# Transposed exponentials through DRAM blocks and VectorE, and a new order of the first weights

The kernel runs on one core of a Trainium2 chip. The metric is the device time of one launch in microseconds (us); lower is better. Every time below is the median of several runs of the same kernel, and all runs were in the fast state (granted TensorE clock between 0.993 and 1.000 of full speed; the clocks below 0.996 are those of two runs of `after_again`). TensorE is PE in the profile, VectorE is DVE, ScalarE is ACT, and SyncE (SP, its queue SPq) only issues DMAs.

## The reference

A block-recurrent cross attention feeds a two-layer network. There are 8 batches and 8 heads of 64, 512 tokens `x` and 32 states per head.

```python
a      = softmax(scale * x @ state.T)      # 512 x 32 per head: every token reads the states
xread  = a @ state
a2     = softmax(scale * state @ x.T)      # 32 x 512 per head: every state reads the tokens
sread  = a2 @ x
t      = concat(xread, sread)              # (8 batches) x 544 rows x 512
h      = t @ w_in                          # 512 x 2048
g      = h * sigmoid(1.702 * h)
out    = g @ w_out                         # 2048 x 512
```

## The kernel before

The two weights arrive as 64-bit words and are turned into 32-bit floats on the chip, in 32 pieces of 512 KB (16 of `w_in`, 16 of `w_out`). Most of that is VectorE's work. For a `w_in` piece two of the steps, the "clamps", are on ACT; for a `w_out` piece all seven are on VectorE.

```python
PIECES = [("i", c, k) for c in range(NFC) for k in range(NPR)] + [("o", f) for f in range(NF)]
...
def round_a(i):
    if i not in power:
        mask(i)                                    # VectorE, and the source of the ACT clamps
    sc = power[i]
    if PIECES[i][0] == "o":
        nc.vector.tensor_scalar(sc, sc, most, least, ALU.min, ALU.max)
        nc.vector.tensor_scalar(sc, sc, -least, 8.0, ALU.add, ALU.mult)
        return
    nc.scalar.activation(out=sc.bitcast(FP32), in_=sc, func=AF.Relu, bias=edge[0], scale=-8.0)
    nc.scalar.activation(out=sc, in_=sc.bitcast(FP32), func=AF.Relu, bias=edge[1], scale=-1.0)
```

`powers_to(n)` does the clamps up to piece n; `rounds(n)` and `round_to(n)` finish pieces.

Batches 0 and 1 run while the weights are still arriving, with plain products: first `M = state @ w_in`, then "up products" `a @ M` with the gelu on ACT (that is `xread @ w_in`, summed over 8 x 32 states rather than 512 columns), and then a "down loop" of 16 steps, one `w_out` piece each. Batches 2 to 7 run later with a two-level Strassen scheme (fewer products, many additions on VectorE) and are TensorE-bound. The first such stage, which multiplies batch 1's gelus by `w_out`, lies between about 166 and 200 us.

The state's own read needs its exponentials `e` transposed. For batches 0 and 1 TensorE did it:

```python
att_s_exp(0, room[:, :NG]); att_s_exp(1, room[:, NG:])     # four 128x512 exponentials on ACT
rounds(1)                                                   # finish one weight piece
att_s_norm(0); att_s_norm(1)                                # 1/sum, and e = e * (1/sum), on VectorE
...
for f in range(NF):                                         # the down loop
    rounds(1)
    round_to(NFC * NPR + f + 1)
    for r in range(SCH):
        down(0, r, [f], out_x[0, r], r == SCH - 1)
    if f == 0:
        for b in range(2):
            for g in range(NG):
                att_eT(b, g)        # 4 TensorE transposes and an ACT copy
    if f == 1:
        att_sread(0); att_sread(1)
        ...
```

Batches 2 to 7 already did it another way: `eT_out` writes the exponentials to DRAM as 32x32 blocks, `eT_in` reads the blocks back at their new places, and `eT_turn` turns each block on VectorE.

## Time and profile before

| | before |
|---|---|
| median time of 3 runs | 708.97 us (708.93 to 709.03) |
| profiled span | 706.9 us |
| first exponential of batches 0 and 1 starts | 73.07 us |
| first product of the TensorE-bound part (`upx<-aT,M`) | 204.43 us |

The last row is my yardstick in every trace: from there on all kernels here do the same work at TensorE's pace, so what it moves by is, within about 0.3 us, what the whole time moves by.

ACT's timeline of the kernel before (start, duration, engine, line, operation, what it writes and reads, and in brackets the idle time before it and who ended it).

```profile
24.52 0.72 ACT L218 ACTIVATE low<-low,edge 128x512 f32<-128x512 int32 x1 [0.33 <-DVE low L207]
...
28.14 0.73 ACT L218 ACTIVATE low<-low,edge 128x512 f32<-128x512 int32 x1
```

Each line is the first clamp of a pair. They are done here, in front of the exponential of batch 1, in time that ACT would otherwise have spent waiting.

### The profile page before, as it was taken

How to read it: one execution, taken by the hardware profiler on the slowest of the kernel's cores; microseconds unless marked ns; L12 is line 12 of the kernel's file. 1: busy time of each engine (PE TensorE's matmuls, PEld its weight loads, DVE VectorE, ACT ScalarE, POOL GpSimd, SP SyncE). 2: the span in 40 equal slices, each digit the busy share in tenths (PEclk: the TensorE clock that was granted, in tenths of full speed). 3: DMA queues.
4: the chain of work that ended last, by engine and by line, in shares of the span. 5: the costliest groups of instructions: out<-in, count | busy, mean ns of one | idle time of the engine just before them, and what ended most of it. 6: DMA issues, size and time to landing. Idle time of an engine off the chain costs nothing.

```text
span 706.9 us, 12667 instructions
## 1 busy us (share of the span) xinstructions
PE 694.9 (98%) x4973; PEld 558.1 (79%) x4975; DVE 602.4 (85%) x1246; ACT 230.8 (33%) x456; POOL 0.8 (0%) x8
## 2 busy tenths in 40 slices
PE   8989999999999999999999999999999999999996
PEld 3433544458998799879988899889987998899995
DVE  6999799999978998799978996899789987888650
ACT  5686520014224413433243423342243124200210
POOL 0000000000000000000000000000000000000000
PEclk9999999999999999999999999999999999999999
DMA  8921246228742384309550765047432940041001
GB/s 230 368 74 54 93 146 154 115 89 206 213 118 37 61 194 145 69 9 206 148 105 1 152 182 120 16 82 199 137 51 48 194 148 16 0 125 57 16 1 29
DMA packets 143914, 77.89 MB, mean 110 GB/s; under 512 B 113904, under 2 KB 127728, under 8 KB 143856
## 3 DMA queue, kind: packets, MB, share of 16 engines
q1 hardware_dynamic: 143856, 77.09, 42.3%
q8 instruction: 39, 0.64, 0.4%
q14 instruction: 19, 0.16, 0.1%
HBM read 61.08 MB, written 15.99 MB: 109 GB/s over the span
## 4 chain that ended last, share of the span: by engine, by line
PE 95%; ACT 2%; DMA 2%; SPq 0%; DVE 0%; issue 0%; DVEq 0%
PE low L689 21%; PE o L1051 17%; PE o L738 14%; PE o L689 10%; PE o L542 8%; PE h L524 7%; PE upx L1051 6%; PE M L320 4%; PE o L585 2%; PE o L320 1%; PE sr L500 1%; PE warm L125 1%; PE upx_sr L1051 1%; DMA out_dram<-osb_sr 1%; DMA xn<-in_x_dram 1%; ACT low L219 1%
## 5 line engine op out<-in xcount | busy, mean ns | idle before, releaser
L1061 DVE TENSOR_TENSOR g<-o,g 128x512 f32<-128x512 f32 (+1 forms) x140 | 88.0, 650 | 51.1 <-PE o L1051 50.1
L738 PE MATMUL o<-w_out,g 128*128 128x256 f32 x448 | 100.6, 381 | 0.0
L738 PEld LDWEIGHTS o<-w_out,g 128*128 128x128 f32 x448 | 84.4, 190 | 16.6 <-issue 5.5
L1058 ACT ACTIVATE g<-g 128x512 f32<-128x512 f32 (+1 forms) x84 | 49.8, 600 | 100.9 <-DVE g L1061 100.9
L1051 PE MATMUL upx<-aT,M 128*128 128x256 f32 x192 | 49.3, 379 | 0.0
L1051 PE MATMUL o<-ta,M 128*128 128x256 f32 x192 | 49.3, 379 | 0.0
L1051 PE MATMUL o<-ta,ms 128*128 128x256 f32 x192 | 48.3, 379 | 0.0
L689 PE MATMUL low<-low,g 128*128 128x128 f32 x336 | 44.4, 275 | 0.0
L689 PEld LDWEIGHTS low<-low,g 128*128 128x128 f32 x336 | 40.9, 192 | 0.0
L460 ACT COPY M<-M 128x512 f32<-128x512 f32 x64 | 33.1, 598 | 22.7 <-PE M L320 22.7
L1051 PEld LDWEIGHTS o<-ta,ms 128*128 128x128 f32 x192 | 36.6, 190 | 4.9
L1051 PEld LDWEIGHTS o<-ta,M 128*128 128x128 f32 x192 | 36.6, 190 | 4.9
L1051 PEld LDWEIGHTS upx<-aT,M 128*128 128x128 f32 x192 | 36.1, 191 | 4.6
L689 PE MATMUL low<-sums,later 128*128 128x128 f32 x280 | 37.0, 275 | 0.0
L689 PEld LDWEIGHTS low<-sums,later 128*128 128x128 f32 x280 | 34.6, 192 | 0.4
L320 PE MATMUL M<-w_in,stT 64*32 64x512 f32 x512 | 31.9, 594 | 0.0
L527 ACT ACTIVATE g<-h 128x512 f32<-128x512 f32 x24 | 14.0, 591 | 54.7 <-PE h L524 54.7
L524 PE MATMUL h<-low,M 128*128 128x512 f32 x64 | 29.6, 597 | 1.5 <-DVE low L408 1.5
L524 PE MATMUL h<-aT,M 128*128 128x512 f32 x64 | 28.7, 599 | 1.4 <-ACT M L460 1.4
L689 PE MATMUL low<-w_out,g 128*128 128x128 f32 x224 | 29.6, 275 | 0.0
L542 PE MATMUL o<-w_out,g 128*128 128x512 f32 x64 | 28.6, 594 | 0.0
L542 PE MATMUL o<-w_out,sums 128*128 128x512 f32 x64 | 28.3, 593 | 0.0
(210 smaller groups left out, 1295.2 us busy)
## 6 DMA issues: line engine op xcount, KB each, us to landing
low<-low SPq DMA_DIRECT2D x78, 256.0 KB, 3.8
later<-in_moe_w_out_dram SPq DMA_DIRECT2D x16, 512.0 KB, 3.6
xn<-in_x_dram SPq DMA_DIRECT2D x28, 256.0 KB, 4.8
low<-low SPq DMA_DIRECT2D x9, 768.0 KB, 4.0
w_out<-in_moe_w_in_dram SPq DMA_DIRECT2D x12, 512.0 KB
xsq<-in_x_dram SPq DMA_DIRECT2D x96, 64.0 KB, 2.3
out_dram<-osb SPq DMA_DIRECT2D x18, 256.0 KB, 3.1
out_dram<-later SPq DMA_DIRECT2D x14, 256.0 KB, 2.2
```

The source lines that it names most:

```text
L125: nc.tensor.matmul(ps, zeros[:, :P], zeros, start=True, stop=True)
L320: nc.tensor.matmul(ps[g][st], A[b]["stT"][rows, st], rhs(rows, j), start=True, stop=True)
L460: nc.scalar.copy(m[:, g], ps[g])
L524: nc.tensor.matmul(hps, lhs[i], rhs[i], start=(i == 0), stop=(i == n - 1))
L527: nc.scalar.activation(out=G[key, f // 2][:, f % 2, :ntok], in_=hps, func=AF.Gelu_apprx_sigmoid)
L542: nc.tensor.matmul(ops, G[key, f // 2][:, f % 2, P * r : P * (r + 1)], w_out[:, f], start=(f == 0), stop=(f == NF - 1))
L585: nc.tensor.matmul(ps[:, r], lhs[f][:, P * r : P * (r + 1)], rhs[:, f], start=(first and r == 0 and f == 0), stop=(f == HF - 1), skip_grou ...
L689: nc.tensor.matmul(ps, lhs[f], rhs[:, f], start=(first and f == 0), stop=(f == QF - 1), skip_group_check=True)
L738: nc.tensor.matmul(ps[:, r], lhs[f][:, P * r : P * (r + 1)], rhs[:, f], start=(r == 0 and f == 0), stop=(f == HF - 1), skip_group_check=True,)
L1051: nc.tensor.matmul(ps[:, k], lhs[i][:, o : o + P], rhs[i], start=(first and k == 0 and i == 0), stop=(i == n - 1), skip_group_check=True,)
L1058: nc.scalar.activation(out=dst, in_=src, func=AF.Gelu_apprx_sigmoid)
L1061: nc.vector.tensor_tensor(out=dst, in0=ps, in1=x, op=ALU.add)
```

## The change

It has two parts, which touch different stretches.

- **The start.** Pieces of `w_in` become (chunk of 512 columns, half of the columns, two row blocks) rather than (chunk, row block), so that two pieces are enough for the first two up products. Some warm-up products go, some gelus are held back, and the clamps of two pieces move behind the exponential of batch 1.
- **The transposes.** Batches 0 and 1 take the road of the later ones: 16 transposes and 4 ACT copies go; 16 DMAs of 128 KB and four 128x512 transposes on VectorE come. The scaling by 1/sum moves from VectorE's `e * (1/sum)` to ACT's copy of the read.

The diff, cut (`...`) to its core:

```diff
-    PIECES = [("i", c, k) for c in range(NFC) for k in range(NPR)] + [("o", f) for f in range(NF)]
+    PIECES = [("i", c, h, k) for c in range(NFC) for h in range(2) for k in range(2)] + [("o", f) for f in range(NF)]
...
-        w = raw[i].rearrange("p (n w) -> p w n", w=2)
+        w = raw[i].rearrange("p (k n w) -> p w k n", k=2, w=2)
...
         nc.vector.reciprocal(out=sm, in_=sm)
-        if b < 2:
-            nc.vector.tensor_scalar(e, e, sm, None, ALU.mult)
...
-    def att_eT(b, g):
-        ...
-        for c in range(SCH):
-            nc.tensor.transpose(ps[:, c], a["e2"][g][0][:, P * c : P * (c + 1)], ident)
-        nc.scalar.copy(a["eT"][:, g], ps)
...
+    att_M(0, 0, h=0)
     powers_to(2)
     round_to(3, 0)
     powers_to(4)
     att_x_norm(0)
-    keep_warm(24)
+    keep_warm(16)
     att_state(1)
     for j in range(NPR):
-        keep_warm(2)
         att_xT(1, j)
     att_scores(1)
-    keep_warm(3)
-    powers_to(4)
-    round_to(NPR, 1)
-    att_M(0, 0)
-    powers_to(NPR + 2)
+    up_x(0, 0, hold=True)
+    up_x(0, 1, hold=True)
+    keep_warm(8, True)
     att_blocks(1)
     att_x_exp(1)
+    gelus()
...
     att_s_exp(0, room[:, :NG])
     att_s_exp(1, room[:, NG:])
+    eT_out(0)
+    eT_out(1)
     rounds(1)
     att_s_norm(0)
     att_s_norm(1)
...
-        if f == 0:
+        if f == 1:
+            eT_in(0)
+            eT_in(1)
+        if f == 4:
             for b in range(2):
                 for g in range(NG):
-                    att_eT(b, g)
-        if f == 1:
+                    eT_turn(b, g)
+        if f == 5:
             att_sread(0)
             att_sread(1)
             ...
```

More of the change, by code (lines that the diff above doesn't have):

```diff
@@ L120, with keep_warm @@
     bank_o = [psO.tile([P, FC], FP32, tag=f"o{i}", name=f"o_{i}") for i in range(4)]
-    def keep_warm(n):
-        ps = psH.tile([P, FC], FP32, tag="h", name="warm")
+    def keep_warm(n, spare=False):
+        ps = att_ps([P, FC], "warm") if spare else psH.tile([P, FC], FP32, tag="h", name="warm")
         for _ in range(n):
@@ L180, in load_weight @@
         if key[0] == "i":
-            _, c, k = key
-            src = w_in_words[P * k : P * (k + 1), 2 * FC * c : 2 * FC * (c + 1)]
-        else:
-            src = w_out_words[P * key[1] : P * (key[1] + 1)]
-        nc.sync.dma_start(raw[i], src)
+            _, c, h, k = key
+            n0 = 2 * FC * c + FC * h
+            src = w_in_words[2 * P * k : 2 * P * (k + 1), n0 : n0 + FC].rearrange("(k p) n -> p k n", k=2)
+            nc.sync.dma_start(raw[i].rearrange("p (k n) -> p k n", k=2), src)
+        else:
+            nc.sync.dma_start(raw[i], w_out_words[P * key[1] : P * (key[1] + 1)])
     least, most = float((1023 - 127) << 20), float((1023 + 128) << 20)
@@ L196, with halved @@
         edge.append(t)
+    def halved(t):
+        return t.rearrange("p (k n) -> p k n", k=2)
     def words(i):
-        w = raw[i].rearrange("p (n w) -> p w n", w=2)
+        w = raw[i].rearrange("p (k n w) -> p w k n", k=2, w=2)
         return w[:, 0].bitcast(U32), w[:, 1]
@@ L204, in mask @@
         _, hi = words(i)
-        sc = low[:, 2 + i % (AHEAD + 1)].bitcast(I32)
+        sc = halved(low[:, 2 + i % (AHEAD + 1)]).bitcast(I32)
         power[i] = sc
@@ L223, in fraction @@
         key = PIECES[i]
-        dst = w_in[key[1]][:, key[2]] if key[0] == "i" else w_out[:, key[1]]
+        if key[0] == "i":
+            _, c, h, k = key
+            dst = w_in[c][:, 2 * k : 2 * k + 2, FC // 2 * h : FC // 2 * (h + 1)]
+        else:
+            dst = halved(w_out[:, key[1]])
         nc.vector.tensor_scalar(dst.bitcast(I32), words(i)[1], 0xFFFFF, 0x100000, ALU.bitwise_and, ALU.bitwise_or)
@@ L366, in att_s_exp @@
         if room is None:
-            room = e2_room[b] = apool.tile([P, NPR, S], FP32, tag="xT", name=f"e2_{b}")
+            room = apool.tile([P, NPR, S], FP32, tag="xT", name=f"e2_{b}")[:, :NG]
+        e2_room[b] = room
         a["e2"] = []
@@ L449, with att_M @@
     turns = {"M": 0}
-    def att_M(b, c, spare=False):
-        m = mpool.tile([P, NG, FC], FP32, tag=f"M{turns['M'] % NFC if b < 2 else c}", name=f"M_{b}_{c}")
-        turns["M"] += 1
-        A[b]["M", c] = m
-        name = f"M_{b}_{c}_"
-        ps = [psH.tile([P, FC], FP32, tag="h", name=name + str(g)) if spare else att_ps([P, FC], name + str(g)) for g in range(NG)]
-        by_state(b, ps, lambda rows, j: w_in[c][rows, j])
+    def att_M(b, c, spare=False, h=None):
+        if not h:
+            A[b]["M", c] = mpool.tile([P, NG, FC], FP32, tag=f"M{turns['M'] % NFC if b < 2 else c}", name=f"M_{b}_{c}")
+            turns["M"] += 1
+        m = A[b]["M", c]
+        n0, n = (0, FC) if h is None else (FC // 2 * h, FC // 2)
+        name = f"M_{b}_{c}_{h}_"
+        ps = [psH.tile([P, n], FP32, tag="h", name=name + str(g)) if spare else att_ps([P, n], name + str(g)) for g in range(NG)]
+        by_state(b, ps, lambda rows, j: w_in[c][rows, j, n0 : n0 + n])
         for g in range(NG):
-            nc.scalar.copy(m[:, g], ps[g])
-    squares = dram.tile([Ns, NG * NB, NPR, Ns], FP32, name="squares")
+            nc.scalar.copy(m[:, g, n0 : n0 + n], ps[g])
+    squares = [dram.tile([Ns, NG * NB, NPR, Ns], FP32, name=f"squares_{i}") for i in range(2)]
     def eT_out(b):
         for j in range(NPR):
-            src = e2_room[b][Ns * j : Ns * (j + 1), :NG].rearrange("n g (t a) -> n (g t) a", a=Ns)
-            nc.sync.dma_start(squares[:, :, j], src)
+            src = e2_room[b][Ns * j : Ns * (j + 1)].rearrange("n g (t a) -> n (g t) a", a=Ns)
+            nc.sync.dma_start(squares[b % 2][:, :, j], src)
     def eT_in(b):
         a = A[b]
-        a["eT"] = apool.tile([P, NG, SCH, P], FP32, tag="eT", name=f"eT_{b}")
-        v = squares.rearrange("n (k i) j a -> i n k (j a)", i=SCH)
+        a["eT"] = apool.tile([P, NG, SCH, P], FP32, tag="e1" if b == 1 else "eT", name=f"eT_{b}")
+        v = squares[b % 2].rearrange("n (k i) j a -> i n k (j a)", i=SCH)
         for i in range(SCH):
@@ L480, in eT_turn @@
         nc.vector.transpose(t, t)
-    def att_eT(b, g):
-        a = A[b]
-        if g == 0:
-            a["eT"] = apool.tile([P, NG, SCH, P], FP32, tag="e1" if b else "eT", name=f"eT_{b}")
-        ps = att_ps([P, SCH, P], f"eT_{b}_{g}")
-        for c in range(SCH):
-            nc.tensor.transpose(ps[:, c], a["e2"][g][0][:, P * c : P * (c + 1)], ident)
-        nc.scalar.copy(a["eT"][:, g], ps)
     def att_sread(b):
@@ L504, in att_sread @@
         sr = apool.tile([P, P], FP32, tag="sr", name=f"sr_{b}", bufs=2)
-        if b < 2:
-            nc.scalar.copy(sr, ps.rearrange("p g d -> p (g d)"))
-        else:
-            for g in range(NG):
-                nc.scalar.activation(out=sr[:, D * g : D * (g + 1)], in_=ps[:, g], func=AF.Copy, scale=a["e2"][g][1])
+        for g in range(NG):
+            nc.scalar.activation(out=sr[:, D * g : D * (g + 1)], in_=ps[:, g], func=AF.Copy, scale=a["e2"][g][1])
         A[b]["sr"] = sr
@@ L518, with gelus, up @@
     G = {}
-    def up(key, f, ntok, lhs, rhs, spare=False):
+    held = []
+    def gelus():
+        for out, hps in held:
+            nc.scalar.activation(out=out, in_=hps, func=AF.Gelu_apprx_sigmoid)
+        held.clear()
+    def up(key, f, ntok, lhs, rhs, spare=False, hold=False):
         hps = att_ps([P, ntok], f"h_{key}_{f}") if spare else psH.tile([P, ntok], FP32, tag="h", name=f"h_{key}_{f}")
@@ L526, in up, with up_x @@
             G[key, f // 2] = free.pop(0)
-        nc.scalar.activation(out=G[key, f // 2][:, f % 2, :ntok], in_=hps, func=AF.Gelu_apprx_sigmoid)
-    def up_x(b, f, spare=False):
+        held.append((G[key, f // 2][:, f % 2, :ntok], hps))
+        if not hold:
+            gelus()
+    def up_x(b, f, spare=False, hold=False):
         c, o = divmod(P * f, FC)
         m = A[b]["M", c]
-        up(b, f, S, [m[:, g, o : o + P] for g in range(NG)], [A[b]["aT"][:, g] for g in range(NG)], spare)
+        up(b, f, S, [m[:, g, o : o + P] for g in range(NG)], [A[b]["aT"][:, g] for g in range(NG)], spare, hold)
     O = {}
@@ L1118, with rounds @@
     nper = FC // P
-    def rounds(n):
-        round_to(done["b"] + n)
+    def rounds(n, ahead=AHEAD):
+        round_to(done["b"] + n, ahead)
     load_weights(2)
@@ L1144, with turn @@
     att_x_norm(0)
-    keep_warm(24)
+    keep_warm(16)
     att_state(1)
     for j in range(NPR):
-        keep_warm(2)
         att_xT(1, j)
     att_scores(1)
-    keep_warm(3)
-    powers_to(4)
-    round_to(NPR, 1)
-    att_M(0, 0)
-    powers_to(NPR + 2)
+    up_x(0, 0, hold=True)
+    up_x(0, 1, hold=True)
+    keep_warm(8, True)
     att_blocks(1)
     att_x_exp(1)
-    up_x(0, 0)
-    up_x(0, 1)
+    gelus()
+    round_to(NPR, 0)
+    att_M(0, 0, h=1)
+    att_M(1, 0, True)
+    powers_to(NPR + 1)
     up_x(0, 2, True)
     up_x(0, 3, True)
-    att_M(1, 0, True)
-    round_to(NPR + 1)
     att_x_norm(1)
-    def turn(b, c, then, n=()):
+    round_to(NPR + 1, 1)
+    def turn(b, c, then, n=(), ahead=(AHEAD,) * nper):
         for i in range(nper):
-            if i == nper - 1 and then:
+            up_x(b, nper * c + i)
+            if i == nper - 2 and then:
                 att_M(*then)
-            up_x(b, nper * c + i)
             if i < len(n):
-                rounds(n[i])
-    turn(1, 0, None, [1, 1, 1])
-    att_M(0, 1)
-    turn(0, 1, (1, 1), [1, 1, 1])
+                rounds(n[i], ahead[i])
+    turn(1, 0, (0, 1, False, 0), [1, 1, 1], (1, 2, 2))
+    up_x(0, nper)
+    att_M(0, 1, h=1)
+    rounds(1)
+    up_x(0, nper + 1)
+    rounds(1)
+    up_x(0, nper + 2)
+    att_M(1, 1)
+    rounds(1)
+    up_x(0, nper + 3)
     round_to(3 * NPR)
@@ L1237 @@
             att_M(1, 3)
-        if f == 2:
+        if f == 6:
             att_srT(0)
             att_srT(1)
-        if f == 2 or f % 2 == 1 and 1 < f < NF - 1:
+        if 5 < f < NF - 3:
             up_x(1, rest.pop(0))
```

## The prediction

> **What bounds the kernel now.** I read the page first: busy shares, the row of slices, the chain that ended last. Then the busy table by stretch, then the timelines of TensorE, VectorE (DVE), ScalarE (ACT) and SyncE over the first 205 us, the only part that the change touches.
>
> ```profile
> PE 694.9 (98%) x4973; PEld 558.1 (79%) x4975; DVE 602.4 (85%) x1246; ACT 230.8 (33%) x456; POOL 0.8 (0%) x8
> ...
> PE 95%; ACT 2%; DMA 2%; SPq 0%; DVE 0%; issue 0%; DVEq 0%
> ...
> 70.00:77.00 7.00, 7.00 (x18) 3.08 (x17) 2.87 (x13) 6.19 (x12) 0.00 (x0) 1.00 0.24 77
> 77.00:100.00 23.00, 22.76 (x218) 11.47 (x217) 22.31 (x48) 7.98 (x18) 0.00 (x0) 1.00 0.41 132
> 100.00:130.00 30.00, 30.00 (x71) 13.34 (x70) 29.13 (x60) 2.39 (x4) 0.00 (x0) 1.00 0.52 130
> 130.00:166.00 36.00, 36.00 (x151) 19.91 (x149) 35.34 (x46) 5.21 (x10) 0.00 (x0) 1.00 0.33 131
> 166.00:200.00 34.00, 34.00 (x362) 31.82 (x355) 32.66 (x85) 10.65 (x27) 0.00 (x0) 1.00 0.80 190
> 200.00:230.00 30.00, 30.00 (x161) 27.01 (x160) 22.98 (x39) 12.13 (x20) 0.00 (x0) 1.00 0.32 69
> ```
>
> The columns of a stretch are its length, then busy us of PE, PEld, DVE, ACT. TensorE has only 12.0 us of idle in the whole span, nearly all before 46.5 us. After about 205 us five batches follow at a TensorE-bound pace (equal stages 75.6 us apart), so whatever the change does by 205 us is carried to the end unchanged. The second thing to see: from 77 to 199 us VectorE is as full as TensorE (97% by this table; its timeline shows no gap with a named releaser). In that region both are bounds, VectorE hidden behind a chain that says "PE".
>
> ```profile
> 73.88 0.15 DVE L378 TENSOR_SCALAR sm<-sm 128x1 f32<-128x1 f32 x1 [3.85 <-ACT e L372]
> 74.07 0.16 DVE L379 RECIPROCAL sm<-sm 128x1 f32<-128x1 f32 x1
> 74.27 0.48 DVE L381 TENSOR_SCALAR e<-e,sm 128x512 f32<-128x512 f32 x1
> ...
> 149.91 2.48 DVE L156 STREAM_TRANSPOSE xsq<-xsq 128x512 f32<-128x512 f32 x4
> ...
> 180.22 0.23 DVE L694 TENSOR_TENSOR later<-low,pu 128x128 f32<-128x128 f32 x1
> ...
> 200.23 0.29 DVE L694 TENSOR_TENSOR pu<-low,pu 128x128 f32<-128x128 f32 x1 [0.97 <-PE low L689]
> ```
>
> VectorE last idles before 73.88, waiting for the exponentials of batches 0 and 1; it next idles at 200.23. So those exponentials start a VectorE run of 126 us. At 180.22 it does an add that TensorE needs (it ends at 180.45, and the product that reuses its bank starts at 180.55; that product's group takes 0.94 us where its neighbours take 0.89). There TensorE has practically no slack left towards VectorE.
>
> **What the Trainium skill says.** "VectorE: DVE Perf Modes", The three transpose paths: VectorE transposes 32x32 blocks only, into SBUF; TensorE does the full 128x128 into PSUM. The trace agrees: the TensorE route needs an ACT copy (588 ns each); the new one needs the blocks placed by DMA. Same page, What auto-detection actually checks: single-source fp32 operations keep the double rate if all is in SBUF and the outermost dimension is even. The split views have outer size 2, so mask and fraction should keep their 0.42 us; only the trace after can show that. "DMA: Bandwidth & Descriptors", Specifications: below 512 B a transfer misses line rate. The 32-word runs of the blocks are 128 B, and this trace's windows while such blocks go out move about 146 GB/s, against 366 to 421 GB/s for weights late in the first 30 us. "ScalarE: Activation LUTs", What ACT_TABLE_LOAD costs: 1283 ns plus a drain for each set switch; the trace has 1283 ns, and exp to gelu starts 2.37 us apart.
>
> **The change, part by part.**
>
> (a) TensorE loses 16 transposes with their copy wait in between:
>
> ```profile
> 81.42 0.45 PE eT L489 x4
> 81.87 0.02 issue
> 81.90 0.59 ACT eT L490
> 82.49 0.04 issue
> 82.53 1.15 PE eT L489 x8
> ```
>
> 83.68 - 81.42 = 2.26 us. The read of the state moves from step 1 of the down loop to step 5; the same work otherwise. Six down steps now follow each other: 3.43 us of TensorE against 3.53 us of VectorE for a w_out piece. Piece 17 would be ready about 1.7 us before its step, and that slack shrinks by 0.1 a step: no stall.
>
> (b) VectorE loses four scalings of e, but not all of their time counts: the last sum arrives from ACT at 75.85, then 0.4 us of small operations, so the next piece starts at 76.25 instead of 77.01: -0.76 us. It gains four 128x512 transposes at the pitch of the row at 149.91 (2.40 us for four). Net +1.64 us, inside the full run.
>
> (c) DMA: 8 writes and 8 reads of 128 KB more. For later batches an issue takes SyncE about 0.7 and 0.6 us, and about 4.5 us pass to landing. The writes are issued from 74.4 to about 80.5; the load of w_out piece 4 queues behind them and lands near 84.5, wanted at 86.8. The reads land near 96, their transposes come at 97.3. Hidden, by 1 to 2 us.
>
> (d) The start. Pieces are now half a chunk's columns by two row blocks, so two pieces suffice for two up products. Walking the engines in program order with measured pitches (clamp pair 1.38 us, gelu 0.48, 128x512 copy 0.53, 128x256 copy about 0.33, w_in piece on VectorE 2.47, up product 1.77): x of batch 1 lands near 20.4 as before; its scores end near 23.6 (before: 25.3); up products (0,0) and (0,1) start at 23.65, behind aT at 23.25. The exponential of batch 1 starts at 27.55 (before: 29.92), gelus end at 31.0, M(1,0) follows, up products (0,2), (0,3) end at 35.65. There batch 1's products start, at 37.46 before: 1.8 us ahead.
>
> But the clamps of pieces 4 and 5, which ACT did in its idle time at 24.5 and 28.1, now come after that exponential: 2 x 1.38 = 2.76 us more ACT work in the region that follows. From 27.55 on ACT has 12 clamp pairs (16.5), 15 gelus (7.2), copies (5.3), exp and table (2.4): 31.4 us, i.e. to 59 if it never waits, and I count about 2.6 us of waits. By this walk the double clamp of pieces 7 and 8 holds gelu (1,2) until 44.5, and product (0,4) starts at 45.25 (46.49 before); (1,4) waits for copies until 54.5 (54.7 before); and product (0,8) starts at 62.8 (62.9 before). So the lead G left when batch 0's last third begins, hence at the exponentials, is about 0.1 us. It could be 1.5 us if my ACT walk is too pessimistic.
>
> **Sum.** TensorE alone would gain 2.26 + G. But VectorE starts its run G earlier and is 1.64 us longer, with about 0.1 us of slack at the add at 180.22. The end moves by 1.64 - 0.1 - G = +1.4 us with G = 0.1: 710.4. The 2.3 us taken from TensorE become waits for VectorE in the first seven-product stage after the down loop.
>
> **Rivals.**
> 1. TensorE stays the bound. For it: the chain names TensorE for 95% and VectorE for 0. Against it: no VectorE gap for 126 us. It would give 708.97 - 2.26 - 0.1 = 706.6, and 705 with a larger G.
> 2. VectorE bounds, but the start keeps its 1.8 us lead because ACT keeps up. For it: the spacing of the clamps looks made for that; ACT had 1 to 3 us of gaps there. Against it: the ACT sum above. It gives 708.97 + 1.54 - 1.8 = 708.7.
> 3. A DMA becomes the bound: piece 4 of w_out or the blocks come late, and each late us goes into VectorE's run. For it: 2 MB more in short runs on one queue. Against it: the margins in (c). It gives 711 to 713.
> 4. The split views lose VectorE's double rate: mask and fraction go from a pitch of 0.34 to about 0.60 us, at least 32 x 0.26 = 8 us over: 717 or more. I give it 3%.
>
> **Range and chances.** The walk gives 710.4; rivals 1 and 2 pull down, rival 3 up. I weight the walk with about 45%, rival 2 with 25%, rival 1 with 17%, rival 3 with 10%: near 709.6. Range 706.5 to 712.0. Two per cent is 14.2 us, more than all of TensorE's idle time, and slower by that much needs rival 4 in full: faster 0.01, same 0.97, slower 0.02.
>
> **What would show it.** Right: VectorE without a gap from about 76 to about 200 us; TensorE waiting 2 to 4 us for VectorE adds (the L694 kind) between 165 and 182 where it waited for none; four e<-e,sm scalings gone, four more eT<-eT transposes near 97 us; the first up product near 23.7 us; ACT nearly full from 38 to 60 us with TensorE waits on gelus and M copies there; the exponentials of batches 0 and 1 within 0.5 us of 73. Wrong: these exponentials more than 1 us earlier (then G is larger and the time is below 709); no TensorE wait near 170 (then rival 1, below 707.5); a gap on VectorE released by a DMA near 87 or 97 us (rival 3); mask rows of 0.6 us or more (rival 4).

## The result

| | before | after |
|---|---|---|
| median of 4 runs each | 709.0 us (708.93 to 709.24) | 711.94 us (711.26 to 712.54) |
| profiled span | 706.9 | 710.0 |
| ratio | | 1.0041, 95% interval 1.0023 to 1.0058 |

A ratio here is the mean time of one kernel's runs over that of the other's in the same rounds, so it is not quite the ratio of the medians. The kernel became 2.9 us slower: "same" by the 2% rule, inside the predicted range and at its upper edge. In the trace the yardstick product moved from 204.43 to 207.40 us, +2.97.

Where TensorE has 2.26 us less to do, it should have ended earlier. The page of the kernel after, then its busy table by stretch:

```profile
PE 694.3 (98%) x4980; PEld 557.0 (78%) x4980; DVE 603.2 (85%) x1246; ACT 229.6 (32%) x458; POOL 0.8 (0%) x8
...
PE 91%; ACT 3%; DMA 3%; DVE 2%; SPq 1%; issue 0%; DVEq 0%
```

```profile
130.00:166.00 36.00, 36.00 (x150) 21.30 (x149) 35.24 (x48) 5.73 (x11) 0.00 (x0) 1.00 0.29 114
166.00:200.00 34.00, 31.96 (x334) 29.05 (x328) 33.42 (x86) 10.58 (x26) 0.00 (x0) 1.00 0.84 198
```

TensorE was busy all of the 34 us from 166 to 200 before; now it idles 2.04 us there, and VectorE, which did 32.66 us of work there, does 33.42. (From the end of the down loop, 152.97 before and 152.62 after, TensorE takes 3.32 us longer to the yardstick; the 2.04 are the part that shows as idle.) VectorE has entered the chain of waits (from 0 to 2%). TensorE's timeline has two waits:

```profile
173.88 1.16 PE L695 MATMUL low<-sums,later 128*128 128x128 f32 x8 [1.77 <-ACT pu L704]
...
177.17 1.16 PE L695 MATMUL o<-sums,spare_M 128*128 128x128 f32 x8 [0.27 <-DVE spare_M L700]
```

Behind the first stand ACT and, behind ACT, VectorE. VectorE's row of maxima in the kernel before, the same row in the kernel after, and ACT's rows after it:

```profile
168.65 0.15 DVE L359 TENSOR_SCALAR mx<-mx 128x1 f32<-128x1 f32 x1
```

```profile
171.92 0.15 DVE L368 TENSOR_SCALAR mx<-mx 128x1 f32<-128x1 f32 x1
```

```profile
172.11 0.69 ACT L382 ACTIVATE e<-o,mx 128x512 f32<-128x512 f32 x1 [0.80 <-DVE mx L368]
...
172.90 0.69 ACT L382 ACTIVATE e<-o,mx 128x512 f32<-128x512 f32 x1
...
173.58 0.26 ACT L704 COPY pu<-low 128x128 f32<-128x128 f32 x1
```

The third product adds to a bank from which ACT must first copy the first product. That copy ends at 173.84, just before the product starts (173.88). In ACT's program it stands behind two exponentials, and these start when VectorE has their maxima (the first at 172.07). VectorE has this row 3.27 us later than before. The second wait is the one through which the chain of waits runs:

```profile
174.79 0.60 DVE g L751
175.38 0.20 DVE pu L700
175.59 0.61 DVE g L751
...
176.22 0.69 DVE later L751
176.91 0.21 DVE spare_M L700
...
177.17 1.16 PE o L695 x8
```

VectorE's additions stand back to back, and the product starts 0.05 us after the last of them. Before the 174.10 addition this chain leads through a load of tokens (6.08 us, landed at 173.55), but VectorE's own timeline has no gap there, and in `et_only` (below) the chain from 163 to 175.5 us is VectorE's rows without a DMA: the load is not the cause. TensorE waits, directly or through ACT, for an engine that has shown no wait for almost 100 us. VectorE's timeline shows how it got there:

```profile
75.63 0.15 DVE L388 TENSOR_SCALAR sm<-sm 128x1 f32<-128x1 f32 x1 [2.56 <-ACT e L382]
...
77.90 0.41 DVE L212 TENSOR_SCALAR low<-later 128x512 int32<-128x512 int32 x1
...
99.06 2.48 DVE L490 STREAM_TRANSPOSE eT<-eT 128x512 f32<-128x512 f32 x4
101.46 0.39 DVE L212 TENSOR_SCALAR low<-later 128x512 int32<-128x512 int32 x1
```

The four transposes take 101.46 - 99.06 = 2.40 us. The next piece (the row at 77.90) starts 3.08 us after the first exponential (74.82), where it started 3.94 us after it before (77.01 against 73.07): the scalings of `e` save 0.86. The balance is +1.54 us. No VectorE row from 72 to 204 us has a DMA as its releaser, so the DRAM round trip itself stayed hidden.

The rest comes from the start, where the exponentials moved from 73.07 to 74.82. TensorE's timeline of the kernel after:

```profile
9.20 0.66 PE L319 MATMUL xT<-ident,xn 128*128 128x128 f32 x4 [0.30 <-DMA xn<-in_x_dram]
...
25.25 3.70 PE L528 MATMUL h<-aT,M 128*128 128x512 f32 x8
...
46.75 1.98 PE L528 MATMUL h<-aT,M 128*128 128x512 f32 x4 [1.66 <-ACT M L470]
...
58.02 3.83 PE L528 MATMUL h<-low,M 128*128 128x512 f32 x8 [0.36 <-ACT g L521]
```

The first row waits for the first tokens, which land 0.94 us later than before in this profile (9.20 against 8.26). The up products do start earlier (25.25 against 27.82), but then TensorE waits 1.66 and 0.36 us for ACT. ACT itself idled earlier, just where the clamps had been:

```profile
29.21 1.06 ACT L404 ACTIVATE e<-e 128x1024 f32<-128x1024 f32 x1 [5.00 <-DVE e L403]
```

### The profile page after: what moved, and what is told of

It reads as the page before. It is cut to its first block, busy times and chain, and to the rows that moved or that the text cites.

```text
span 710.0 us, 12712 instructions
## 1 busy us (share of the span) xinstructions
PE 694.3 (98%) x4980; PEld 557.0 (78%) x4980; DVE 603.2 (85%) x1246; ACT 229.6 (32%) x458; POOL 0.8 (0%) x8
## 4 chain that ended last, share of the span: by engine, by line
PE 91%; ACT 3%; DMA 3%; DVE 2%; SPq 1%; issue 0%; DVEq 0%
PE low L695 21%; PE o L1057 17%; PE o L744 13%; PE o L695 10%; PE o L548 8%; PE upx L1057 6%; PE h L528 5%; PE M_None L329 4%; PE o L591 2%; DMA xn<-in_x_dram 2%; PE o L329 1%; PE sr L500 1%; PE upx_sr L1057 1%; DMA out_dram<-osb_sr 1%; ACT low L224 1%; ACT low L223 1%
## 5 line engine op out<-in xcount | busy, mean ns | idle before, releaser
L470 ACT COPY M<-M_None 128x512 f32<-128x512 f32 x60 | 31.0, 598 | 20.0 <-PE M_None L329 20.0
L329 PE MATMUL M_None<-w_in,stT 64*32 64x512 f32 x480 | 30.7, 593 | 0.1
L704 ACT COPY pu<-low 128x128 f32<-128x128 f32 x21 | 5.6, 266 | 67.8 <-PE low L695 63.5
```

The lines of the kernel that those rows point to most:

```text
L329: nc.tensor.matmul(ps[g][st], A[b]["stT"][rows, st], rhs(rows, j), start=True, stop=True)
L470: nc.scalar.copy(m[:, g, n0 : n0 + n], ps[g])
```

## The experiments

All of them ran in three groups of four, each group on another chip, five timed runs each, with nine runs of the kernel before beside every group (medians 708.81, 708.84 and 708.77).

My theory was that the end is set by the later of two chains that were level before: TensorE's and VectorE's, both full from the exponentials to the first Strassen stage. The rivals were that the loss is in the start alone, that it is in the DMAs (late blocks, late weights, or the shorter rows in which the weights are now loaded), or that the late landing of the tokens made it.

### One part at a time

`et_only` is the kernel before with every transposes hunk of the diff; `start_only` is the kernel after with those hunks taken back.

> The kernel before with only the second half of the change: exponentials of batches 0 and 1 through DRAM blocks and turned by VectorE, the state read at step 5. Theory (VectorE's run from the exponentials to the first seven-product stage is the bound there, 1.64 us longer by this part, 0.3 us of it swallowed): 1.3 us slower than before, 710.3 us, TensorE waits of 3 to 4 us near 170 us. Rival (TensorE is the bound): 2.3 us faster, 706.7 us, no such waits.

> The changed kernel with the exponentials turned by TensorE again as before: only the new order of pieces, the clamps and the held gelus are left. Theory (the new start makes the exponentials of batches 0 and 1 about 1.75 us later and everything after them with it): 1.5 to 1.75 us slower than before, 710.6 us. Rival (the start gains as it was meant to, and the loss is all in the exponentials' way): equal to or up to 2 us faster than before, 707 to 709 us.

Measured: `et_only` 710.46 (710.34 to 711.02), ratio 1.0023 (1.0011 to 1.0036), so +1.65. `start_only` 709.32 (709.15 to 709.48), ratio 1.0006 (0.9993 to 1.0019), so +0.51, which the interval doesn't tell from nothing; its trace does (below). It misses the expected 1.5 to 1.75, of which 0.94 was the late landing of the tokens in one profile (below, too). Both parts lose, and the transposes lose most. The busy table of `et_only` shows the same idle on TensorE with the old start:

```profile
166.00:182.00 16.00, 13.91 (x110) 13.22 (x109) 15.72 (x39) 5.14 (x12) 0.00 (x0) 1.00 0.91 198
```

The kernel before was busy for all 16.00 of these 16 us. So the 2.09 us of waits come from the transposes, not from the start. (3 to 4 us were expected; as in the kernel after, not all of the loss shows as idle.)

### Taking VectorE's two costs apart

`before_turns` leaves everything as before and only gives VectorE the four transposes; their output is not used, since the TensorE transposes are still there.

```diff
+        if f == 4:
+            for b in range(2):
+                for g in range(NG):
+                    eT_turn(b, g)
```

`et_no_turn` is `et_only` without the four transposes (wrong: the blocks stay unturned. The check of the result can't tell whether the blocks are turned).

> The kernel before with nothing but four more 128x512 VectorE transposes at step 4 of the down loop, on a tile that nothing reads any more (the result stays right). Theory (VectorE's run is full up to the first seven-product stage, with 0.3 us to spare): 2.4 - 0.3 = 2.1 us slower, 710.9 us, with TensorE waits of about 2 us near 172 us. Rival (TensorE is the bound, VectorE has room): 708.8 us, no waits.

> As et_only without the four VectorE transposes (the read of the state is wrong on purpose; the DRAM traffic and the later read stay). Theory (the four transposes are what makes et_only slow): VectorE's run is 0.76 us shorter than before and TensorE 2.26 us, so TensorE waits about 1.2 us near 170 us and the end comes 0.8 to 1.1 us earlier than before, 707.9 us. Rival (the DRAM traffic costs it): 710.4 us as et_only.

Measured: `before_turns` 711.08 (710.68 to 711.22), ratio 1.0031 (1.0018 to 1.0043), +2.31: 2.40 us of VectorE work that nobody waits for cost nearly their whole length. TensorE's waits are 1.15 and 0.27 us, where about 2 were expected; the rest of the 1.99 us in the trace lies in products that follow each other more slowly from 172.89 to 177.18. `et_no_turn` 707.80 (707.70 to 708.04), ratio 0.9986 (0.9973 to 0.9998), -0.97: TensorE was relieved of 2.26, but the time fell only by about the 0.86 that VectorE was relieved of.

### Relieving VectorE in the kernel before

`before_defer` finishes two weight pieces rather than one before the sums, so that VectorE works through its 3.85 us wait for the exponentials; the rest is untouched.

```diff
-    rounds(1)
+    rounds(2)
     att_s_norm(0)
     att_s_norm(1)
```

> The kernel before with w_out piece 17 rounded ahead of the small sums and scalings, in VectorE's 3.8 us of waiting for the exponentials; nothing else. Control for et_defer2: theory (in the kernel before TensorE has no gap to lose, so an earlier VectorE gains nothing): 708.8 us within 0.2. Rival (the deferral itself gives the 1.8 us of et_defer2): 707.0 us.

Measured: 708.79 (708.58 to 708.87), ratio 0.9999 (0.9986 to 1.0011). The room appears on VectorE, where the kernel before had no named wait before 200 us (1.26, 0.35, 0.96 and 0.51 us between 136 and 173), but the time stays. With TensorE's work as before, a freer VectorE is worth nothing.

### Relieving both

The new road takes TensorE's 2.26 us away; the wait for the exponentials has room for VectorE's extra work. `et_defer` (from `et_only`) and `after_defer` (from the kernel after) put one piece ahead of the block writes and move the sums into the down loop:

```diff
     att_s_exp(1, room[:, NG:])
+    rounds(1)
     eT_out(0)
     eT_out(1)
-    rounds(1)
-    att_s_norm(0)
-    att_s_norm(1)
...
         if f == 1:
             eT_in(0)
             eT_in(1)
+            att_s_norm(0)
+            att_s_norm(1)
```

> As et_only, but the small sums of the exponentials are taken up by VectorE only after w_out piece 19, and the blocks go out behind the load of w_out piece 4, so that VectorE does not stand waiting for the exponentials. Theory (VectorE's run is the bound; here it starts 4 us earlier): TensorE becomes the bound and keeps its 2.26 us: 706.7 us, no waits near 170 us. Rival (the extra DMA traffic or TensorE itself makes et_only's time): no different from et_only.

> The changed kernel with the same deferral. Theory: the stall near 170 us goes, and what stays is TensorE's own position at the end of the down loop, 152.62 against 153.14 us before: 0.5 us faster than before, 708.5 us, 3.4 us faster than the changed kernel. Rival: within 0.5 us of the changed kernel, 711.9 us.

Measured: `et_defer` 708.84 (707.54 to 709.28), ratio 0.9997 (0.9984 to 1.0009): a miss of 2.1 us. `after_defer` 707.98 (707.61 to 708.55), ratio 0.9987 (0.9973 to 1.0001), half a microsecond below what I expected, but near it by luck: the expected 152.62 came from the profile with the late tokens, and compares the start of a product with the end of one (153.14; the start is 152.97). In its own trace TensorE is at 151.41 there, 1.56 ahead of before, and the yardstick only 0.95 ahead: VectorE still sets the end. VectorE's timeline of `et_defer` (its profiled run was the slowest of the five, 709.28) shows what ate the gain:

```profile
87.02 0.43 DVE L207 TENSOR_SCALAR low<-later 128x512 int32<-128x512 int32 x1 [1.84 <-DMA later<-in_moe_w_out_dram]
...
94.55 1.30 DVE L479 STREAM_TRANSPOSE eT<-eT 128x512 f32<-128x512 f32 x2 [0.39 <-DMA eT<-squares]
...
97.54 1.31 DVE L479 STREAM_TRANSPOSE eT<-eT 128x512 f32<-128x512 f32 x2 [1.69 <-DMA eT<-squares]
```

VectorE was ready for the first of these pieces at 85.18, 5.3 us earlier than in `et_only` (90.45), and met transfers that had not moved: a weight load that SyncE had issued only after the eight block writes, then the blocks themselves. Together 3.92 us. The DRAM road was hidden in the change only because VectorE was late. (`after_defer` has a single such wait, 1.03 us for the blocks at 96.39.)

`et_defer2` therefore does two pieces first, so that the weight load is issued ahead of the writes, and reads the blocks back one step earlier:

```diff
-    rounds(1)
+    rounds(2)
     eT_out(0)
     eT_out(1)
...
-        if f == 1:
+        if f == 0:
             eT_in(0)
             eT_in(1)
+        if f == 1:
             att_s_norm(0)
             att_s_norm(1)
```

> As et_defer, with the blocks going out behind two weight loads, and read back one step earlier, because in et_defer VectorE waited 3.9 us in all for a late weight load and for the blocks. Theory (VectorE's run is the bound, and those waits gave the 4 us back): waits under 1 us in all, TensorE the bound, no stall near 170 us, 706.7 us. Rival (TensorE's 2.26 us are not to be had): 708.8 us as et_defer.

Measured: 707.03 (707.01 to 707.23), ratio 0.9976 (0.9963 to 0.9988), -1.81; in the trace the yardstick moves by -2.07, nearly all of the 2.26. Its busy table:

```profile
166.00:182.00 16.00, 16.00 (x137) 15.77 (x137) 14.02 (x36) 4.80 (x12) 0.00 (x0) 1.00 0.92 212
```

TensorE is full again, and this time VectorE is the one with room (14.02 of 16). The six kernels with the old start now read as one rule. All entries are differences from the kernel before: what was added to or taken from TensorE and VectorE, then where VectorE's row of maxima (at 168.65 before) and the yardstick lie in the trace, and the time:

| kernel | TensorE's work | VectorE's work | VectorE's row | yardstick | time |
|---|---|---|---|---|---|
| `before_turns` | 0 | +2.40 | +2.28 | +1.99 | +2.31 |
| `et_only` | -2.26 | +1.54 | +1.66 | +1.33 | +1.65 |
| `et_no_turn` | -2.26 | -0.86 | -0.59 | -0.90 | -0.97 |
| `et_defer` | -2.26 | relieved, then 3.92 of waits | +0.54 | +0.22 | +0.03 |
| `before_defer` | 0 | relieved | -1.63 | +0.14 | +0.02 |
| `et_defer2` | -2.26 | relieved | -3.66 | -2.07 | -1.81 |

The end follows the later of two: TensorE's own work, or VectorE's row less a slack. In the first four kernels it is VectorE's row, and the slack is 0.29 to 0.33 us in each; in the last two it is TensorE's work (the tokens land 0.13 and 0.09 us later in these traces than before). The kernel after (+3.27 and +2.97), `after_again` (+2.44 and +2.14) and `after_defer` (-0.63 and -0.95) have the same slack. Yardstick (one run) and time (median of five) differ by up to 0.3 us.

### The start

`after_again` is the kernel after, unchanged, in a later group; `before_2k` is the kernel before with the new, 2 KB rows of the weight loads and nothing else (the weights come out permuted, so its result is wrong).

> The changed kernel once more, unaltered, on the chip of this call. In its first profile x of batch 0 reached TensorE at 9.20 us; in two later kernels with the same loads it was there at 7.9 us. If the late landing comes and goes from run to run or chip to chip, its two parts (1.65 and 0.5 us alone) add up to 710.7 to 711.0 us here. If it belongs to the changed kernel, 711.9 us again.

> The kernel before, with each w_in load taking rows of 2 KB from 256 rows instead of 4 KB from 128, as the changed kernel's loads do (the weights land in wrong places, so the result is wrong on purpose; all times stay). If shorter rows delay x at the start: x at 9.2 us instead of 8.3 and 0.9 us slower, 709.7 us. If they do not: 708.8 us within 0.3.

Measured: `after_again` 711.10 (710.79 to 713.24), ratio 1.0041 (1.0028 to 1.0055), 0.1 above the first of the two forecasts. `before_2k` 708.67 (708.44 to 708.76), ratio 0.9997 (0.9985 to 1.001): the shorter rows cost nothing. The first row of `after_again` that waits for tokens:

```profile
8.16 0.66 PE L319 MATMUL xT<-ident,xn 128*128 128x128 f32 x4 [0.26 <-DMA xn<-in_x_dram]
```

So the late landing (9.20) belonged to one profile, not to the change. Everything behind it moves rigidly with it. I call its start x0:

| kernel | x0 | first exponential | difference |
|---|---|---|---|
| before | 8.26 | 73.07 | 64.81 |
| `et_only` | 8.34 | 73.13 | 64.79 |
| after | 9.20 | 74.82 | 65.62 |
| `after_again` | 8.16 | 73.86 | 65.70 |
| `start_only` | 7.86 | 73.50 | 65.64 |
| `start_clamps` (next) | 8.00 | 72.83 | 64.83 |

The new start costs 0.8 us in every trace of it, whenever the tokens land; only `start_clamps` has it back.

`start_clamps` is `start_only` with the clamps of the two pieces back in ACT's idle time:

```diff
     keep_warm(8, True)
+    powers_to(NPR + 2)
     att_blocks(1)
     att_x_exp(1)
```

> As start_only, but the clamps of w_in pieces 4 and 5 are done before the exponential of batch 1, in ACT's idle 5 us there, as the kernel before did. Theory (ACT's 2.8 us more of clamps behind that exponential ate the new start's lead): 1.5 us faster than start_only, 707.8 us, the first product on the second chunk at about 43.8 instead of 45.4 us. Rival (the lead is lost to TensorE's or VectorE's own work): as start_only, 709.3 us.

Measured: 708.55 (708.48 to 708.65), ratio 0.9996 (0.9984 to 1.0009), 0.77 below `start_only`, where I had expected 1.5. The wait of TensorE at the fifth up product of batch 0, in `start_only` and then in `start_clamps`:

```profile
45.44 1.98 PE L542 MATMUL h<-aT,M 128*128 128x512 f32 x4 [1.65 <-ACT M L471]
```

```profile
44.77 1.98 PE L542 MATMUL h<-aT,M 128*128 128x512 f32 x4 [0.80 <-ACT M L471]
```

The place of the clamps is worth 0.81 us in the trace (65.64 against 64.83), which is all that the new start had lost. It isn't worth more because half of the wait stays: with two clamp pairs less, ACT idles 1.12 us for a product at 38.07 and 0.61 us for a VectorE mask at 41.12, so there it isn't ACT's amount of work that holds the product back but the order in which masks, clamps and copies follow each other. That reading is from the timeline; I ran nothing that changes that order. The mended start is level with the old one: the 0.29 us by which `start_clamps` is below the kernel before is what its tokens landed earlier (8.00 against 8.26).

### Both repairs in the kernel after

`both_defer2` is the kernel after with the edits of `et_defer2` and `start_clamps`.

> The changed kernel with both mends: clamps of pieces 4 and 5 ahead of the exponential of batch 1, and the deferral and the order of loads of et_defer2. Theory (both halves gain once they are off VectorE's and ACT's full stretches): et_defer2's 707.0 less the 0.3 us that the mended start was ahead of before: 706.7 us. Rival (the halves interfere again): 707.5 us or more.

Measured: 706.76 (706.67 to 706.80), ratio 0.997 (0.9956 to 0.9984), correct. It beats the kernel before by 2.01 us and the kernel after by more than 4. In its trace neither TensorE nor VectorE has a named wait from 130 to 197 us, and the yardstick is at 202.20, 2.23 before that of the kernel before. The new order of the pieces adds 0.3 us at most to what `et_defer2` reached with the old one, within what runs of different groups differ by.

## Why the prediction was right, and where its sum was off

The class and the mechanism of the transposes were right. That the number is inside the range is luck, by 0.06 us: the tokens' late landing in the first profile (+0.94), which was not foreseen, and step (d) below pushed it to the edge, and of the nine timed runs of the kernel after two lie above 712.0 (712.54 and 713.24). By its steps:

- **What bounds the kernel.** That VectorE is a second bound, hidden behind a chain that says "PE" 95%, is what `before_turns` shows directly: 2.40 us of work on it that nobody uses cost 2.31.
- **(a)** TensorE's 2.26 us are real: `et_defer2` gets 2.07 of them in the trace. In the change they became 2.04 us of waits, in the stage and of the size that the prediction named. VectorE is the engine behind both, but only the 0.27 us are a wait for one of the additions that it named; the 1.77 us run through ACT's exponentials and copy.
- **(b)** +1.64 was +1.54 (-0.86 and +2.40).
- **(c)** Hidden was right for the change itself. How much margin was left is not shown; with VectorE 5.3 us earlier, in `et_defer`, it was used up and 3.92 us of waits came out.
- **The slack** of 0.1 us was 0.3 (0.29 to 0.33 in the seven traces above that VectorE bounds). It had been read from one addition and one product that took 0.05 us longer.
- **(d) is the term that failed.** The prediction put the lead at the exponentials at G = +0.1. It is -0.83, measured from the tokens' landing (65.64 against 64.81). Counted that way, scores of batch 1 were to end 15.3 us after x0 (23.6 less the 8.26 of the profile before), and ended after 16.1 (before: 17.0). In `start_only` ACT clamps a piece before it copies the state of batch 1, and the transposes of x wait for that copy, 0.82 us, though the warm-up products between them are gone: the copy is 12.15 us after x0, as before (12.13). No run moved that copy, so this part is read from the timelines; `start_clamps` still has the wait (0.76 us) and won its 0.81 us further on. Later the gelu that holds TensorE at 58.02 costs 0.36 us again. In between the walk's intervals held: from the first up product to the fifth it said 21.60 us (23.65 to 45.25), and 21.50 were measured (25.25 to 46.75). Two of the prediction's own signs failed with G: the first up product (25.25, not 23.7) and the exponentials (74.82, not within 0.5 us of 73).

With the measured terms, the sum is 1.54 - 0.3 + 0.83 = +2.1 us; the trace of `after_again` has +2.14, and its time is +2.26. With the landing of the first profile (+0.94) it is +3.0, and that trace has +2.97. The four runs of the first measurement lie between 711.26 and 712.54; only one of them has a trace.

- **The rivals.** Rival 1 (TensorE alone) fell with the waits near 170; rival 2 (the lead survives) fell with exponentials at x0 + 65.6; rival 3 (a late DMA) isn't in the change, though it was waiting behind it; rival 4 (slow split views) fell with masks of 0.41 us: the split views are as fast as the old ones. The walk gave 710.4; weighting in rivals 1 and 2 pulled the forecast to 709.6, away from the result. The argument was better than the blend.
- **A reading.** The 2.37 us from exp to gelu are from start to start. From the end of the exponential (30.98) to the gelu (32.29) are 1.31 us, of which the table load takes 1.28: in this trace no drain shows beside the load.

Open: why the tokens landed 0.94 us late in one profile (the rows of the loads are not it; the 15 timed runs of `start_only`, `start_clamps` and `both_defer2` spread by no more than 0.33 us in each), and the 713.24 of one run of `after_again`, which had the lowest clock of all runs (0.993).

## What to carry to other kernels

Before you take work off the engine that the chain names, look for a second engine that is full over the same stretch: the end follows the later of the two, and moving work between them pays only if the receiver has a wait to put it into. A wait for something else (here 3.85 us for the exponentials) is that place, if you move independent work into it. When an engine then comes earlier, check the transfers that were hidden only because it was late, and issue the one that it needs first ahead of the bulk.

## What the Trainium skill lacked or had wrong

- "Perfetto Trace Analysis", Identifying the Most-Contended Engine: take the engine with the highest occupancy and optimize it first. By the page's measures (VectorE's occupancy, 85%, against TensorE's busy weight loads, 79%) that would be VectorE; by the chain of waits (95%) it would be TensorE. Neither answer was enough here: relieving VectorE alone changed the time by 0.02 us (`before_defer`), relieving TensorE by 2.26 us while adding 1.54 to VectorE cost 1.65 (`et_only`), and relieving both gave 1.81 (`et_defer2`). The page speaks of regimes in which the bound changes over time; it lacks the case of two engines that are level at once.
- "VectorE: DVE Perf Modes", The three transpose paths: it compares the paths by duration (311 ns on VectorE, 390 on TensorE for 128x128 bf16), by block size and by where the result goes. Here the TensorE path took 2.26 us for sixteen 128x128 fp32 blocks with an ACT copy in between, the VectorE path 2.40 us for the same amount plus 16 DMAs; what decided was which engine had room. The page has no durations of fp32 transposes.
- "DMA: Bandwidth & Descriptors", Issuing engines are not separate DMA queues: it calls the time to initiate a DMA "usually small relative to the DMA itself". That holds for one of these blocks (in the kernel after an issue took SyncE 0.81 us for the eight writes and 0.61 us for the eight reads of batches 0 and 1, medians, with 4.7 us from issue to landing). The section lacks that eight of them in a row, 6.83 us, hold up what is queued behind, and in `et_defer` a weight load behind eight writes came 1.84 us late.
